# Reordering the set-up of a short-convolution and max-out feed-forward kernel

## The chip, the core and the metric

The kernel runs on one core of a Trainium2 chip. A core has five engines, each with its own instruction queue that it works off in order: TensorE (PE in the profile; its weight loads are listed apart as PEld), VectorE (DVE), ScalarE (ACT), GpSimd (POOL) and SyncE (SP). Here SP issues nearly all DMAs; ACT issues one. Engines wait for each other and for DMAs through semaphores. The metric is the device time of one launch in microseconds, and less is better.

## What is computed

An input x of 8 sequences, 4160 tokens and 192 channels passes a causal convolution of 7 taps whose weights are a softmax over the taps, one set for each of 8 heads of 24 channels. The result goes, token by token, through a feed-forward layer that takes the maximum of three products and multiplies it by an output matrix.

```python
w = np.exp(w - np.max(w, axis=-1, keepdims=True))
w = w / (np.sum(w, axis=-1, keepdims=True) + 1e-09)          # [8 heads, 7 taps]
out = np.einsum('hk,bskhg->bshg', w, x_unf)                  # causal convolution, 7 taps
...
h = np.maximum(np.maximum(x @ w1, x @ w2), x @ w3)           # x: 33280 x 192, w: 192 x 768
return (h @ w_out).astype(np.float32)                        # w_out: 768 x 192
```

## The kernel before

The 33280 tokens are cut into 65 blocks of 512. The maximum of three is made of two: the kernel forms the differences `wd` = w1 - w3 and w2 - w3, multiplies the convolved tokens by them, takes max(relu(first), second), and adds the w3 part through a product of w3 and w_out (`m16`), so PE has two instead of three large products for a block.

All order is written out by hand (the framework's scheduler is off): each engine does its instructions in the order in which the program names them. After a set-up for the weights and for four blocks, a loop over the blocks 2 to 64 does for each: the first-layer products (`l1`), the maximum (`top`: relu on ACT at line 490, maximum on DVE at line 491), the output products of the block before (`st2`), the convolution of a later block, and its transposes and loads.

The set-up, in the order of the program, with the names that the change touches:

- The filter `wk` is loaded by a DMA that ACT issues (line 230). SP issues x block 0 (`load_x(0)`, two DMAs), the first 256 columns of the weights (`load_wa`, `load_wb`), x block 1, the rest of the weights, `wos` (w_out) and x blocks 2 and 3.
- `keep_warm(n)` issues n matmuls on zeros (line 252).
- The softmax is made of a maximum on DVE (`wneg`), an exp on ACT (line 269; the engine loads a function table before it), and a sum, a reciprocal and a product on DVE, which write `line`, the taps in a row of zeros.
- From `line`, 38 small matmuls (line 283) build the banded matrix `band`, which ACT and DVE copy out of PSUM (line 287).
- Blocks 0 to 3 ("dense") are convolved by `conv_dense`: 80 matmuls (line 378) of `xz`, an fp16 copy of x in two zero-padded versions, against `band`; the halves n = 0 and n = 1 are cast to `yd` by two engines (line 383). `cast_dense` (line 211) makes `xz` out of the loaded `xf`.
- `zero_x(t)` zeroes partitions 32 to 63 of the x buffers of blocks 4, 5 and 6, which later loads fill only in part: on ACT by a copy of zeros (line 137), or on the engine that it is given by a memset (line 134). SP's loads into a buffer wait for it.
- `make_wd(n, j0, j1)` forms the difference number n for some of the six groups of 128 columns (line 302). `copy_w3` copies half of w3 to the other 64 partitions (line 306); the difference number 2, which holds the last 64 channels, needs it. `cross_wd` copies halves of `wd` (line 313).
- `l1_dense(tiles, parts)` issues the products of blocks 0 and 1: "F" are those of the first 128 channels (four full-array matmuls for two tiles; they need the ACT half of `yd`), "H" the third products, over the last 64 channels (half-array matmuls, which run in pairs; they need the other half of `yd` and `wd` number 2). `tops` follows with relu and maximum.

After the set-up, lines 676 to 704 give the order around the change: differences, `conv_dense(0)`, zero fill and loads of blocks 4 to 6, `copy_w3`, difference 2, x1's casts, F of block 0, `conv_dense(1)`, H of block 0 and its `tops`, then H and F of block 1, and so on with the next column groups. In `conv_dense(1)` DVE casts half 0 and ACT half 1, half 1 first.

Of the kernel before, what the change touches and what calls it, by code (L numbers as in the profile page):

```python
# [10 lines left out]
FP32 = mybir.dt.float32  # L11
FP16 = mybir.dt.float16
AXX = mybir.AxisListType.X
AF = mybir.ActivationFunctionType
# [14 lines left out]
def kernel(  # L29
# [83 lines left out]

    QUADS = 13
    assert (NB - QUADS) % 4 == 0
    xin, xbuf, XBUF, loaded = {}, [], 7, set()

    def get_x(t):

        if not 0 <= t < NB or t in xin:  # L120
            return
        if t < XBUF:
            xbuf.append(const.tile([P, NR, D], FP32, name=f"xf_{t}"))
        xf = xbuf[t % XBUF if t < NDENSE + XBUF else NDENSE + (t - NDENSE - XBUF) % 3]
        assert all(v[0] is not xf for v in xin.values())
        xin[t] = [xf, 0, ()]

    def zero_x(t, q0=0, q1=NR, eng=None):

        if t >= NDENSE:  # L130
            get_x(t)
        xf = xbuf[t]
        if eng is not None:
            eng.memset(xf[TOK:HALF, q0:q1, :], 0.0)
            return
        zero = idle[TOK:HALF, 0:D]
        nc.scalar.copy(out=xf[TOK:HALF, q0:q1, :],  # L137
                       in_=bass.AP(tensor=zero.tensor, offset=zero.offset,
                                   ap=[list(zero.ap[0]), [0, q1 - q0], [1, D]]))

    def load_x(t, eng=nc.sync):
        if not 0 <= t < NB:
            return
        loaded.add(t)
        get_x(t)
        xf = xin[t][0]
        if t < NDENSE:
            todo = [(0, c[3], c[1] * SEQ + c[2], i) for i, c in enumerate(chunks_of[t])]
        else:
            todo = [(HALF * (i // NR) + (0 if s else LAP), KR if s else TOK,  # L150
                     b * SEQ + s - (LAP if s else 0), i % NR) for i, (b, s) in enumerate(rows_of(t))]
        parts = []
        i, n = 0, len(todo)
        row = [c[2] for c in todo]
        while i < n:
            k = i
            while k + 1 < n and todo[k + 1][:2] == todo[i][:2] and row[k + 1] - row[k] == row[i + 1] - row[i]:
                k += 1
            step = row[i + 1] - row[i] if k > i else 0
            p0, rlen, _, q0 = todo[i]  # L160
            q1 = todo[k][3] + 1
            src = bass.AP(tensor=x.tensor, offset=row[i] * D,
                          ap=[[D, rlen], [step * D, q1 - q0], [1, D]])
            eng.dma_start(out=xf[p0:p0 + rlen, q0:q1, :], in_=src)
            if parts and parts[-1][0] == rlen:
                parts[-1] = (rlen, parts[-1][1], q1)
            else:
                parts.append((rlen, q0, q1))
            i = k + 1
        xin[t] = [xf, todo[0][0], parts]  # L170
# [28 lines left out]
    xz = {t: [const.tile([P, NQ, D], FP16, name=f"xz_{t}_{v}") for v in range(2)] for t in range(2)}  # L199
    xz[2], xz[3] = xz[0], xz[1]  # L200

    def cast_dense(t, copies, slots_=range(CYC // 32)):
        xf, _, parts = xin.pop(t)
        for v, copy in enumerate(copies):
            if copy is None:
                continue
            for s in slots_:
                cut = GRP * (32 * s // GRP + 1)
                a, b = (32 * s, cut) if v == 0 else (cut, 32 * s + 32)
                for (rl, q0, q1) in parts:  # L210
                    copy(  # L211
                        out=xz[t][v][0:rl, q0:q1, :].rearrange("p q (k c) -> p q k c", c=CYC)[:, :, :, a:b],
                        in_=xf[0:rl, q0:q1, :].rearrange("p q (k c) -> p q k c", c=CYC)[:, :, :, a:b])
# [14 lines left out]

    wk = const.tile([NHEAD, KW], FP32)
    nc.scalar.dma_start(out=wk[:], in_=weight)  # L230
    wos = const.tile([P, NJ, D], FP32)
    load_x(0)
    load_wa(slice(0, PW))
    load_wb(slice(0, PW))
    load_x(1)
    load_wa(slice(PW, 2 * PW))
    load_wb(slice(PW, DFF))
    load_wa(slice(2 * PW, DFF))
# [9 lines left out]
    def keep_warm(n, pool=psw, tag="w"):  # L248

        ps = pool.tile([P, NBLK], FP32, tag=tag, name="idle")  # L250
        for _ in range(n):
            nc.tensor.matmul(ps[:], lhsT=idle[:, 0:P], rhs=idle[:], start=True, stop=True)
# [6 lines left out]
    nc.vector.memset(line[:], 0.0)  # L259
    for v in range(2):  # L260
        nc.vector.memset(xz[0][v][:], 0.0)
    band = const.tile([P, NHEAD, BAND_W], FP16)
    nc.vector.memset(band[:], 0.0)
    keep_warm(5, psp, "p")
    wexp = const.tile([NHEAD, KW + 1], FP32)
    nc.vector.memset(wexp[:], 1e-9)
    wneg = const.tile([NHEAD, 1], FP32)
    nc.vector.reduce_max(out=wneg[:], in_=wk[:], axis=AXX, negate=True)
    nc.scalar.activation(out=wexp[:, 0:KW], in_=wk[:], func=AF.Exp, bias=wneg[:])  # L269
    wrec = const.tile([NHEAD, 1], FP32)  # L270
    nc.vector.reduce_sum(out=wrec[:], in_=wexp[:], axis=AXX)
    nc.vector.reciprocal(out=wrec[:], in_=wrec[:])
    zero_x(4)
    nc.vector.tensor_scalar_mul(out=line[:, 31:31 + KW], in0=wexp[:, 0:KW], scalar1=wrec[:])
    for v in range(2):
        nc.vector.memset(xz[1][v][:], 0.0)
    cast_dense(0, (nc.vector.tensor_copy, nc.vector.tensor_copy))
    CUT = 28
    for lo, hi, copy in ((0, CUT, nc.scalar.copy), (CUT, WIN, nc.vector.tensor_copy)):
        bps = psq.tile([32, hi - lo + 3, NHEAD], FP32, tag="q", name=f"band_{lo}")  # L280
# [5 lines left out]
        for a in range(4):  # L286
            copy(out=band[32 * a:32 * a + 32, :, 32 * a + lo:32 * a + hi],  # L287
                 in_=bps[:, 0:hi - lo, :].rearrange("p c h -> p h c"))
    zero_x(5)
    keep_warm(3, psp, "p")  # L290


# [7 lines left out]
    def make_wd(n, j0, j1, eng=nc.vector):  # L300
        f = slice(P * j0, P * j1)
        eng.tensor_sub(out=wd[:, n, f], in0=ws[:, n, f], in1=w3s[:, n // 2, f])

    def copy_w3(copy, j0, j1):
        f = slice(P * j0, P * j1)
        copy(out=w3s[HALF:P, 1, f], in_=w3s[0:HALF, 1, f])

    def cast_w3(j0, j1):
        f = slice(P * j0, P * j1)
        nc.gpsimd.tensor_copy(out=w3h[:, :, f], in_=w3s[:, :, f])  # L310

    def cross_wd(i, copy):
        copy(out=wd[HALF * i:HALF * (i + 1), NC, :], in_=wd[HALF * (1 - i):HALF * (2 - i), i, :])
# [52 lines left out]
    def conv_dense(t, copies, pools=((None, None),) * 2, order=(0, 1)):  # L366


        yd = dense[t] = ydp.tile([P, NC, NBLK], FP16, tag="yd", name=f"yd_{t}")
        for n in order:  # L370
            slots_ = ((0, 1, 2, 3), (4, 5, 4, 5))[n]
            pool, tag = pools[n]
            ps = (pool or psw).tile([P, NBLK], FP32, tag=tag or "w", name=f"D{n}_{t}")
            for (q, b, row_lo, rlen, lo, hi, cc) in chunks_of[t]:
                for v in range(2):
                    for g, s in enumerate(slots_):
                        h = (32 * s + 31 * v) // GRP
                        nc.tensor.matmul(  # L378
                            ps[32 * g:32 * g + 32, lo:hi],
                            lhsT=xz[t][v][0:rlen, q, 32 * s:32 * s + 32],  # L380
                            rhs=band[0:rlen, h, cc:cc + hi - lo],
                            start=(v == 0), stop=(v == 1), tile_position=(0, 32 * g))
            copies[n](out=yd[:, 2 * n, :], in_=ps[:])
# [129 lines left out]
    def l1_dense(tiles, parts="FH"):  # L513

        meet()
        for n, part in enumerate(parts):
            for t, j, pools in tiles:
                for i, (pool, tag) in enumerate(pools):
                    if (t, j, i) not in open_ps:
                        open_ps[t, j, i] = pool.tile([P, NBLK], FP32, tag=tag, name=f"l{tag}{i}_{t}_{j}")  # L520
                        begun.discard((t, j, i))
                    if part == "F":
                        a, b = wd[:, i, P * j:P * (j + 1)], dense[t][:, 0, :]
                    else:
                        a, b = w_of(i, NC - 1, j), y_all(t, i, NC - 1)
                    nc.tensor.matmul(open_ps[t, j, i][:], lhsT=a, rhs=b,  # L526
                                     start=(t, j, i) not in begun, stop=(t, j, i) in begun)
                    begun.add((t, j, i))

    def tops(*tiles):  # L530
        for t, j in tiles:
            top(t, j, (open_ps[t, j, 0], open_ps[t, j, 1]))
# [143 lines left out]
    GP = nc.gpsimd.tensor_copy  # L676
    make_wd(0, 0, 2)
    make_wd(1, 0, 2)
    zero_x(6, 4, NR, nc.vector)
    conv_dense(0, (ACT, DVE))  # L680
    zero_x(6, 0, 4)
    for t in range(NDENSE, XBUF):
        load_x(t)
    copy_w3(DVE, 0, 2)
    make_wd(2, 0, 2)
    cast_dense(1, (GP, ACT), (1, 2, 0))
    l1_dense([(0, 0, PQ), (0, 1, PQ)], "F")
    cast_w3(0, 2)
# [2 lines left out]
    for n in range(NC):  # L691
        make_wd(n, 4, 6, nc.gpsimd)
    cast_w3(2, 6)
    conv_dense(1, (DVE, ACT), order=(1, 0))
    make_wd(0, 2, 4)
    make_wd(1, 2, 4)
    cross_wd(0, GP)
    GP(out=wo[:], in_=wos[:])
    l1_dense([(0, 0, PQ), (0, 1, PQ)], "H")
    tops((0, 0), (0, 1))  # L700
    l1_dense([(1, 0, WW), (1, 1, WW)], "HF")
    tops((1, 0), (1, 1))
    l1_dense([(0, 2, PQ), (0, 3, PQ)], "FH")
# [130 lines left out]
```

## Time and profile before

| | us |
|---|---|
| median of 3 runs | 454.24 (454.09 to 456.25) |
| the profiled execution | 454.51 |
| its span, first to last instruction | 452.70 |
| PE busy in the span | 446.8 (99%) |
| DVE, ACT, POOL busy | 356.5, 320.0, 202.9 |

By stages, from the view of busy times in stretches of the span:

| stretch, us | what it holds | PE busy | DVE | ACT | POOL | DMA share |
|---|---|---|---|---|---|---|
| 0 to 7.29 | softmax, band, matmuls on zeros | 4.83 | 4.79 | 4.54 | 1.01 | 0.57 |
| 7.29 to 10.96 | conv 0, F of block 0 | 3.60 | 3.15 | 3.52 | 1.36 | 1.08 |
| 10.96 to 22.66 | conv 1, products of blocks 0 and 1 | 11.70 | 8.71 | 9.06 | 9.96 | 0.97 |
| 22.66 to 31.18 | conv 2 and 3, block 2 | 8.12 | 5.14 | 5.79 | 5.48 | 0.68 |
| 31.18 to 452.70 | the loop | 418.60 | 334.75 | 297.07 | 185.12 | 0.69 |

The busy time of an engine says how much of a stretch it spent in instructions, not whether the end of the stretch waited for it; for that the chain of waits and the timeline are read, whose lines give start, duration, engine, line, operation, tiles and, in brackets, the idle time before and what ended it. Tile names in the lines are output<-inputs; "x5" is a count of merged instructions.

### The profile page before, as it was taken

The page shows a single profiled execution, that of the slowest core. Times are in us where ns is not written, and L with a number is a line of the kernel's source. Part 1 is how long each engine was busy: PE and PEld are TensorE (multiplying, and loading weights), DVE is VectorE, ACT ScalarE, POOL GpSimd, SP SyncE. Part 2 cuts the span into 40 slices and gives each one's busy share as a digit, 9 for nine tenths or more (in the row PEclk, how much of TensorE's full clock was granted, in tenths as well). Part 3 has the DMA queues.
Part 4 walks back from the last instruction along what each step waited for, and adds up shares of the span by engine and source line. Part 5 has one row for each costly group of instructions (what it writes and reads, how often), then busy time and mean ns, then how long its engine had stood idle before and what let it go on. Part 6 is the DMA issues. An engine that isn't in the chain of part 4 may idle for free.

```text
span 452.7 us, 18493 instructions
## 1 busy us (share of the span) xinstructions
PE 446.8 (99%) x7702; PEld 412.6 (91%) x7702; DVE 356.5 (79%) x617; ACT 320.0 (71%) x604; POOL 202.9 (45%) x226
## 2 busy tenths in 40 slices
PE   7999999999999999999999999999999999999997
PEld 3569999999999999999999999999999999999996
DVE  7768778878878787887878788887878788787775
ACT  7767767767777676777767777776767777776664
POOL 2864836556454534645263464535346452505000
PEclk9999999999999999999999999999999999999999
DMA  7969997596875869587685949657594776535223
GB/s 205 231 178 166 199 205 195 146 206 180 169 180 147 168 129 207 138 176 185 118 190 141 210 117 184 177 136 186 133 206 124 178 189 118 117 89 104 59 72 106
DMA packets 127987, 72.03 MB, mean 159 GB/s; under 512 B 52064, under 2 KB 127711, under 8 KB 127903
## 3 DMA queue, kind: packets, MB, share of 16 engines
q1 hardware_dynamic: 127743, 70.75, 68.3%
q8 instruction: 60, 0.98, 1.0%
q14 instruction: 24, 0.20, 0.1%
q10 hardware_dynamic: 160, 0.10, 0.1%
HBM read 33.28 MB, written 25.56 MB: 130 GB/s over the span
## 4 chain that ended last, share of the span: by engine, by line
PE 97%; ACT 1%; DMA 0%; DVE 0%; issue 0%; ACTq 0%
PE po L567 36%; PE lq L503 31%; PE lp L503 22%; PE G L357 3%; PE lw L526 1%; PE lp L526 1%; PE D L378 1%; PE po L625 0%; PE po L598 0%; DMA wk<-in_weight_dram 0%; PE lq L526 0%; ACT xf L137 0%; ACT band L287 0%; ACT L269 0%; PE pm L337 0%; PE band L283 0%
## 5 line engine op out<-in xcount | busy, mean ns | idle before, releaser
L491 DVE TENSOR_TENSOR h<-r,lq 128x512 f16<-128x512 f16 x384 | 263.0, 686 | 85.1 <-ACT r L490 77.3
L567 PE MATMUL po<-wo,h 64*128 64x192 f16 x3024 | 329.8, 243 | 0.0
L490 ACT ACTIVATE r<-lp 128x512 f16<-128x512 f32 x384 | 229.0, 597 | 114.3 <-PE lp L503 100.8
L503 PE MATMUL lp<-yp,wd 64*128 64x512 f16 x1098 | 295.6, 376 | 0.0
L503 PE MATMUL lq<-yp,wd 64*128 64x512 f16 x1098 | 295.5, 376 | 0.0
L567 PEld LDWEIGHTS <-h 64*128 64x128 f16 x3024 | 240.9, 94 | 6.3 <-issue 4.1
L503 PEld LDWEIGHTS <-wd 64*128 64x128 f16 x2268 | 177.7, 94 | 10.6 <-issue 0.2
L194 POOL CAST x<-xf 103x768 f16<-103x768 f32 x122 | 97.5, 827 | 106.6 <-DMA xf<-in_x_dram 93.0
L567 PE MATMUL po<-m,yp 64*128 64x192 f16 x720 | 141.0, 243 | 0.0
L420 POOL COPY yp<-yp 64x1536 f16<-64x1536 f16 (+1 forms) x62 | 89.6, 1445 | 96.2 <-DMA yp<-ys 75.9
L575 DVE TENSOR_TENSOR o<-a,po 128x384 f32<-128x384 f32 x126 | 69.0, 547 | 0.0
L567 PEld LDWEIGHTS <-yp 64*128 64x128 f16 x720 | 66.3, 94 | 0.5
L574 ACT COPY a<-po 128x384 f32<-128x384 f32 x126 | 59.5, 472 | 0.0
L397 ACT CAST ys<-G 128x384 f16<-128x384 f32 x61 | 26.3, 482 | 9.5 <-PE G L357 9.4
L397 DVE CAST ys<-G 128x384 f16<-128x384 f32 x61 | 31.0, 550 | 0.0
L357 PE MATMUL G<-x,band 39*32 39x192 f16 (+2 forms) x1152 | 17.3, 234 | 0.0
L357 PEld LDWEIGHTS <-band 39*32 39x32 f16 x1152 | 10.7, 91 | 5.2 <-issue 4.7
L503 PE MATMUL lp<-yd,wd 64*128 64x512 f16 x36 | 9.7, 376 | 0.0
L503 PE MATMUL lq<-yd,wd 64*128 64x512 f16 x36 | 9.7, 376 | 0.0
L526 PEld LDWEIGHTS <-wd 128*128 128x128 f16 (+1 forms) x48 | 3.2, 98 | 5.7 <-issue 2.4
L211 POOL CAST xz<-xf 112x160 f16<-112x160 f32 (+2 forms) x15 | 4.1, 319 | 7.7 <-DMA xf<-in_x_dram 7.7
L378 PEld LDWEIGHTS <-xz 112*32 112x32 f16 x320 | 4.6, 107 | 2.7 <-issue 1.0
(74 smaller groups left out, 98.2 us busy)
## 6 DMA issues: line engine op xcount, KB each, us to landing
xf<-in_x_dram SPq DMA_DIRECT2D x113, 234.0 KB
out_dram<-o SPq DMA_DIRECT2D x62, 384.0 KB
xf<-in_x_dram SPq DMA_DIRECT2D x7, 204.8 KB
xf<-in_x_dram SPq DMA_DIRECT2D x3, 420.0 KB
ws<-in_moe_w_dram SPq DMA_DIRECT2D x8, 128.0 KB
yp<-ys SPq DMA_TRANSPOSE x62
out_dram<-o SPq DMA_DIRECT2D x5, 192.0 KB
wos<-in_moe_w_out_dram SPq DMA_DIRECT2D x1, 576.0 KB
```

The costliest lines, as they stand in the source:

```text
L194: nc.gpsimd.tensor_copy(out=x16s[t0][0:K, :, :, u, r, :].rearrange("p h j c -> p j h c"), in_=xf[0:K, 4 * r:4 * r + 4, :].rearrange("p j ( ...
L357: nc.tensor.matmul(G[2 * (k // per) + i][TOK * j:TOK * (j + 1), k % per, :], lhsT=band[row, h, HALF * i + LAP:HALF * i + KR], rhs=x16s[t0] ...
L378: nc.tensor.matmul(ps[32 * g:32 * g + 32, lo:hi], lhsT=xz[t][v][0:rlen, q, 32 * s:32 * s + 32], rhs=band[0:rlen, h, cc:cc + hi - lo], star ...
L397: copy(out=slots[t][:, i % 2, :, :, GRP * h0:GRP * (h0 + per)].rearrange("p u r (h c) -> p h (u r) c", c=GRP), in_=G[i][:].rearrange("p h ...
L420: nc.gpsimd.tensor_copy(out=yp[HALF * i:HALF * (i + 1), 1, :, :, :, :].rearrange("p i u k n -> p (i u k n)"), in_=yp[HALF * (1 - i):HALF * ...
L490: nc.scalar.activation(out=r[:], in_=ps[0][:], func=AF.Relu)
L491: nc.vector.tensor_max(out=hs[t][:, j, :], in0=r[:], in1=ps[1][:])
L503: nc.tensor.matmul(ps[i][:], lhsT=w_of(i, c, j), rhs=y_all(t, i, c), start=(n == 0), stop=(n == NC - 1))
L526: nc.tensor.matmul(open_ps[t, j, i][:], lhsT=a, rhs=b, start=(t, j, i) not in begun, stop=(t, j, i) in begun)
L567: nc.tensor.matmul(ps[b0, i][:, s % 2, :], lhsT=a, rhs=b, start=first, stop=last)
L574: nc.scalar.copy(out=a[:], in_=ps[s - 1, 0][:])
L575: nc.vector.tensor_add(out=outs[t][:, s - 1:s + 1, :], in0=a[:], in1=ps[s - 1, 1][:])
```

## The change

Six things move; what is computed stays.

1. A one-element exp on ACT stands before the real one, right behind the issue of the `wk` load, so that the function table is loaded there. The memset of `band` and `keep_warm(5)` are named after the real exp.
2. x block 1 is loaded by a DMA of ACT, after the exp, instead of by SP between two groups of weights.
3. The buffers of blocks 4 and 5 and half of block 6's are zeroed by GpSimd memsets instead of by ACT copies and a DVE memset; one of the two `xz` versions of block 1 is zeroed by GpSimd too.
4. x block 0 is cast in two parts, chunks 0 and 1 and then 2 to 4, as its two DMAs bring them: twelve casts instead of six.
5. `copy_w3` for the first columns goes from DVE to GpSimd and, with difference number 2, ahead of `conv_dense(0)`.
6. H of block 0 and its `tops` go ahead of `conv_dense(1)`; the cast of `wo` on GpSimd goes ahead of `cross_wd(0)`.

```diff
-        if t < XBUF:
-            xbuf.append(const.tile([P, NR, D], FP32, name=f"xf_{t}"))
+    xbuf = [const.tile([P, NR, D], FP32, name=f"xf_{t}") for t in range(XBUF)]
...
-    def cast_dense(t, copies, slots_=range(CYC // 32)):
-        xf, _, parts = xin.pop(t)
+    def cast_dense(t, copies, slots_=range(CYC // 32), qs=(0, NQ)):
+        xf, _, parts = xin[t]
+        parts = [(rl, max(a, qs[0]), min(b, qs[1])) for rl, a, b in parts if a < qs[1] and b > qs[0]]
+        if qs[1] == NQ:
+            xin.pop(t)
...
     nc.scalar.dma_start(out=wk[:], in_=weight)
+    warm = const.tile([1, 1], FP32)
+    nc.vector.memset(warm[:], 0.0)
+    nc.scalar.activation(out=warm[:], in_=warm[:], func=AF.Exp)
     wos = const.tile([P, NJ, D], FP32)
     load_x(0)
     load_wa(slice(0, PW))
     load_wb(slice(0, PW))
-    load_x(1)
...
-    band = const.tile([P, NHEAD, BAND_W], FP16)
-    nc.vector.memset(band[:], 0.0)
-    keep_warm(5, psp, "p")
     wexp = const.tile([NHEAD, KW + 1], FP32)
...
     nc.scalar.activation(out=wexp[:, 0:KW], in_=wk[:], func=AF.Exp, bias=wneg[:])
+    band = const.tile([P, NHEAD, BAND_W], FP16)
+    nc.vector.memset(band[:], 0.0)
+    keep_warm(5, psp, "p")
...
-    zero_x(4)
+    load_x(1, nc.scalar)
     nc.vector.tensor_scalar_mul(out=line[:, 31:31 + KW], in0=wexp[:, 0:KW], scalar1=wrec[:])
-    for v in range(2):
-        nc.vector.memset(xz[1][v][:], 0.0)
-    cast_dense(0, (nc.vector.tensor_copy, nc.vector.tensor_copy))
+    for t in (4, 5):
+        zero_x(t, eng=nc.gpsimd)
+    nc.gpsimd.memset(xz[1][0][:], 0.0)
+    nc.vector.memset(xz[1][1][:], 0.0)
+    zero_x(6, 4, NR, nc.gpsimd)
+    GP = nc.gpsimd.tensor_copy
+    cast_dense(0, (nc.vector.tensor_copy,) * 2, qs=(0, 2))
+    cast_dense(0, (nc.vector.tensor_copy,) * 2, qs=(2, NQ))
...
-    zero_x(5)
     keep_warm(3, psp, "p")
...
-    zero_x(6, 4, NR, nc.vector)
+    copy_w3(GP, 0, 2)
+    make_wd(2, 0, 2)
     conv_dense(0, (ACT, DVE))
...
-    copy_w3(DVE, 0, 2)
-    make_wd(2, 0, 2)
     cast_dense(1, (GP, ACT), (1, 2, 0))
...
+    l1_dense([(0, 0, PQ), (0, 1, PQ)], "H")
+    tops((0, 0), (0, 1))
     conv_dense(1, (DVE, ACT), order=(1, 0))
     make_wd(0, 2, 4)
     make_wd(1, 2, 4)
+    GP(out=wo[:], in_=wos[:])
     cross_wd(0, GP)
-    GP(out=wo[:], in_=wos[:])
-    l1_dense([(0, 0, PQ), (0, 1, PQ)], "H")
-    tops((0, 0), (0, 1))
```

## The prediction

> **What bounds the kernel now.** I read the page first: span, busy shares, slices.
>
> ```profile
> span 452.7 us, 18493 instructions
> PE 446.8 (99%) x7702; PEld 412.6 (91%) x7702; DVE 356.5 (79%) x617; ACT 320.0 (71%) x604; POOL 202.9 (45%) x226
> PE   7999999999999999999999999999999999999997
> ```
>
> TensorE (PE) is busy 99% of the span; only the first and the last slice are below 9. The change touches nothing after block 1, so only the set-up, the first 14 us, can give or lose time, and whatever shift reaches PE there is carried to the end. Next I read the chain of waits in order of time, for that stretch:
>
> ```profile
> 0.75 1.69 DMA wk<-in_weight_dram
> 2.50 1.28 ACT L269
> 3.80 0.31 ACT wexp L269
> 4.50 0.23 DVE line L274
> 4.78 0.94 PE band L283 x28
> ...
> 7.14 1.48 ACT xf L137
> 8.64 0.59 ACT yd L383
> 9.27 0.58 PE lp L526
> ```
>
> The filter weights land, ScalarE (ACT) only then loads its exp table (1.28 us), computes exp, VectorE (DVE) makes `line`, PE makes the band. At 7.14 a zero fill of an x buffer on ACT (1.48) stands in front of the cast `yd` that block 0's first products wait for. Last, the timeline by engine:
>
> ```profile
> 7.29 1.91 PE L378 MATMUL D<-band,xz 112*32 112x103 f16 x80
> 10.08 0.63 PE L526 MATMUL lp<-yd,wd 128*128 128x512 f16 x1
> 10.96 1.11 PE L378 MATMUL D<-band,xz 112*32 112x103 f16 x80
> 11.65 0.59 ACT L383 CAST yd<-D 128x512 f16<-128x512 f32 x1 [0.78 <-PE D L378]
> 13.18 1.41 PEld L526 LDWEIGHTS <-wd 128*128 128x128 f16 x8 [0.64 <-issue]
> 14.06 0.38 PE L526 MATMUL lp<-yd,wd 128*128 128x512 f16 x1
> ```
>
> The same 80 convolution matmuls take 1.91 us at 7.29 and 1.11 at 10.96; one 128x512 product takes 0.63 at 10.08 and 0.38 at 14.06. So PE runs at half speed up to about 10.8 (the clock row shows full speed from the start; the durations contradict it). I measure the shift at 13.18, the first full-array product of block 1: from there PE has no idle time before 28.28.
>
> **The change part by part.** *Table early.* The load depends on nothing once a one-element exp stands in front: it starts when ACT has issued the wk load (0.75+0.58 = 1.33) and ends at 2.61; the one-element exp, at most the 0.30 of the real one, ends by 2.9. wk has landed at 2.44, the maximum takes 0.14, so the real exp runs about 2.85 to 3.15 instead of 3.80 to 4.10. The band memset (0.51) now fills DVE's wait and ends at 3.15. From exp to `line` the rows take 0.62: 4.10 to 4.72, so 3.15 to 3.75. Gain 0.95.
>
> *x0 cast in two parts.* Six casts at 0.15 apart (0.92 in all) become twelve of half the size; by the spread of 0.182 (80 elements) to 0.266 (240) nearly all of it is fixed cost, so about 1.43, or 0.5 more. One memset of xz moves from DVE to GpSimd (POOL): 0.46 less. The two cancel: DVE still needs about 2.5 us from `line` to the band casts that conv 0 waits for (4.72 to 7.23). Conv 0 could start at 6.35 instead of 7.29, if nothing blocks DVE.
>
> *Zero fills on POOL.* ACT loses 1.47 and 1.48, the second one on the chain; DVE loses 0.70 (L134). POOL gets four memsets at 1.7, where it was idle until 9.39. Price by POOL's own memsets: 0.10 for 128x1, 0.21 for 128x128, 0.25 for 7x192, so 0.105 plus 0.76 ns an element: 1.27 twice, 0.83 (960), 0.69 (768), with gaps 4.25; POOL is free at about 5.95. Bounds: 0 extra, if all stays under its idle time, and 1.2 ns an element (the 64x512 copy, 0.61), which ends at 7.6. Behind them wait the w3 copy (half of 0.61) and, in DVE's order, the third difference `wd` and the cast of conv 0's second half; those are due only at 8.2, so either end is covered.
>
> *What POOL and DVE do to each other.* The trace shows one pair:
>
> ```profile
> 23.98 0.37 DVE L389 COPY yd<-yd 64x512 f16<-64x512 f16 x1 [2.37 <-ACT yd L383]
> 24.38 0.29 DVE L389 COPY yd<-yd 64x512 f16<-64x512 f16 x1
> 22.61 1.60 POOL L194 CAST x<-xf 103x768 f16<-103x768 f32 x2
> ```
>
> The first copy, while a POOL cast runs until 24.21, takes 0.37; its equal with POOL idle 0.29. It ends 0.14 after POOL's cast. L306's copy at 10.01 (0.38) also ends 0.14 after POOL's last xz cast (10.25). So such DVE operations appear to wait for the POOL operation in progress. The x0 casts (4.2 to 5.7) now fall into POOL's memsets. Bounds: 0, and all four memsets first: casts from 5.95 to 7.4, band casts, conv 0 at 8.1. I take one wait of 0.1, as in the rows, for each of four memsets: 0.4; conv 0 at 6.75. The Trainium skill (SBUF — State Buffer, "Who interferes with whom") says that a two-port DVE operation and a GpSimd operation exclude each other, the later one blocking fully. It speaks against this change: by that rule alone conv 0 would stand anywhere up to the 8.1 above.
>
> *x1 issued by ACT.* One DMA issue, 0.58, goes behind exp: 3.15 to 3.73; behind it ACT's band casts wait for PE until about 4.75, so it is hidden (0.58 on the path if not). SP loses the step from 5.06 to 5.69: every later weight, wos and x load is issued 0.63 earlier. x1 took 4.2 us from issue to its first use (5.06 to 9.39, a wait for that DMA), so it lands near 7.4.
>
> *Clock.* Before, PE paused from 3.52 to 4.78 and the clock rose about 6 us after it resumed. Now the pause is 3.55 to 3.8. Bounds: 10.8 as before, if something else than the pause set it, and before conv 0. If so short a pause does not count, work is continuous from 1.26 and the same 6.0 us end at 7.3, which I take. The Trainium skill (TensorE: Matmul & The Clock Gate, "The HAM clock gate") gives a free-running window of 3.4 us that must be busy; one window before 10.8 is 7.4, and with its phase unknown the rise would lie between 4.7 and 8.1; the sum would move by 0.4 at most. No row here shows the phase.
>
> *Third products (H) of block 0 ahead of conv 1.* Same PE work, new waits. Then: conv 0 6.75 to 8.1 (slow to 7.3), ACT's cast 7.7 to 8.3, block 0's first products (F) 8.35 to 9.2 (4 matmuls, 0.216 apart), DVE's cast done 8.9, H 9.3 to 9.73. ACT: zero fill 0.83 to 9.19, x1 casts 0.8 to 10.0; conv 1 9.95 to 11.05. Now r0, r1 (1.08) stand ahead of conv 1's cast on ACT: 10.0 to 11.1, cast to 11.7, so block 1's H starts at 11.75 with PE idle 0.7, where before H of block 0 filled that time. DVE: two maxima (1.28) from 10.6, its conv 1 cast 11.85 to 12.5, F of block 1 at 12.5 against 13.18. The sum: **0.7 gained**; 1.0 without the 0.4 at the casts.
>
> *Where it could stick.* POOL's first difference waits for weights until 13.40 and ends, a fourth of 2.79 later, at 14.1; its user on PE comes at 15.05, 0.9 of cover, plus the 0.63 of SP. POOL's x2 casts end half-way through 19.22 to 22.46, at 20.8, conv 2 starts at 22.66. wo is cast before its copy now; 19.28 against 20.59. All wider than 0.7. The rest of the kernel keeps its order, its loads follow PE.
>
> The profiled execution took 454.51, 1.81 more than its span of 452.70; the median 454.24 lies 0.27 below. 452.70 - 0.7 + 1.81 - 0.27 gives 453.5.
>
> **The rivals.** *B, the clock rises no sooner* (0.25). For it: 8-row band matmuls may not count as work. Conv 0 6.35 to 8.3, F slow to 10.06, H 10.15, conv 1 11.1, F of block 1 at 13.3 (+0.1), or 0.3 later with DVE's waits: what the front gains the new order gives back. 454.4.
>
> *C, slower: POOL's memsets hold off the x0 casts* (0.12). For it: the two copies above; against: those waits were of 0.1. Place: DVE between `line` and band. Conv 0 at 8.1, PE idle 6.4 to 8.1, longer than the pause before, and the clock rises about 6 us after, at 14.1. Slow conv 0 to 10.0, F to 11.75, H to 12.7, conv 1 to 14.6, then cast and H: F of block 1 at 15.8, 2.6 late: 456.8. It decides from a conv 0 later than about 7.4.
>
> *D, the clock is full before conv 0 and DVE is never held* (0.15). Conv 0 6.35 to 7.46, F at 7.7, H 8.65, conv 1 9.3, F of block 1 at 11.75: 1.4 gained; 2.2 if ACT's x1 casts and r0, r1 come free sooner. 452.0 to 452.8.
>
> *The table load comes no sooner* would leave 0.95 of it out; against it: nothing of ACT stands ahead. It is inside B.
>
> **How the numbers follow.** Likeliest is A, the sum, with 0.48: 453.5, its own range 452.9 to 454.2. B 0.25, D 0.15, C 0.12. The range to 8 in 10 takes D and B whole with their unknown costs and leaves C out: 452.0 to 455.6. A measurement of this kernel can tell about 0.5% (2.3 us) from no change: faster means below 451.97, the lower end of D and luck, 0.12; slower above 456.5, C and a tail of B, 0.12; same 0.76.
>
> **What would show it.** Table load at about 1.3; `line` near 3.75; conv 0 near 6.75 (7.4 or later: C); conv matmuls turning from 24 to 14 ns apart within conv 0 (not until 10.8: B); x0 casts on DVE longer than 0.2 while POOL's memsets run; ACT's conv 1 cast behind r0 and r1, PE idle before block 1's H; steady blocks at the same length as before. Wrong altogether would be a change of the pace after 31 us.

## The result, and the profile after

| | before | after |
|---|---|---|
| median, us | 454.56 (453.66 to 456.25, 16 runs) | 456.22 (455.73 to 457.82, 16 runs) |
| ratio | | 1.0035, 95% interval 1.0023 to 1.0047 |
| the profiled execution | 454.51 | 457.82 |
| its span | 452.70 | 456.0 |

The change costs about 1.6 us where 0.7 us of gain were forecast. The loss is below the 0.5% that the prediction called no change, but its interval holds neither 1.000 nor the forecast. The profiled execution is the slowest of the 16, so its trace shows more loss (3.3 us of span) than the median has; below, sizes of whole kernels are taken from medians, places and single waits from traces.

First the page of the kernel after: the span, the busy line of PE, its row of forty slices, and a row of the DMA queues (packets, MB, share) that will matter.

```profile
span 456.0 us, 18500 instructions
PE 448.7 (98%) x7702; PEld 412.6 (90%) x7702; DVE 358.0 (79%) x621; ACT 317.1 (70%) x603; POOL 208.1 (46%) x231
PE   7899999999999999999999999999999999999997
q8 instruction: 60, 0.98, 1.0%
```

The second slice of PE (11.4 to 22.8 us) now shows 8: PE stands idle later in the set-up than before. The timeline of the kernel after, by engine:

```profile
1.38 1.28 ACT L235 ACT_TABLE_LOAD   x1 [1.38 <-PEq L825]
...
1.73 2.69 POOL L133 MEMSET xf<- 32x1536 f32 x2
...
2.37 0.35 ACTq L163 DMA_DIRECT2D xf<-in_x_dram  x1
...
3.46 0.98 DVE L278 TENSOR_SCALAR line<-wexp,wrec 8x7 f16<-8x7 f32 x1
...
4.11 2.67 DVE L213 CAST xz<-xf 112x96 f16<-112x96 f32 x12
4.47 0.90 POOL L281 MEMSET xz<- 128x960 f16 x1
...
5.43 0.75 POOL L133 MEMSET xf<- 32x768 f32 x1
...
7.47 1.91 PE L386 MATMUL D<-band,xz 112*32 112x103 f16 x80 [0.39 <-DVE band L296]
...
12.79 0.37 PE L534 MATMUL lp<-yd,wd 64*128 64x512 f16 x1 [1.37 <-DVE yd L391]
...
13.33 1.11 PE L386 MATMUL D<-band,xz 112*32 112x103 f16 x80
...
14.81 3.36 PE L534 MATMUL lw<-yd,wd 64*128 64x512 f16 x8 [0.38 <-ACT yd L391]
...
17.97 0.53 PE L534 MATMUL lp<-yd,wd 128*128 128x512 f16 x1
```

Read it in order. The table load is early, as meant. Then `line` takes 0.98 us for 56 numbers; it ends at 4.44, just after POOL's second memset (1.73 + 2.69 = 4.42). The twelve x0 casts take 2.67 us beside the two other memsets. So conv 0 starts at 7.47, later than the 7.29 of before. H of block 0 follows only at 12.79, conv 1 at 13.33 (10.96 before), and the next full-array products after block 1's at 17.97 (14.06 before).

What stood in front of 12.79 is in the chain of waits of the kernel after, in order of time (start, duration, what):

```profile
4.43 6.58 DMA ws<-in_moe_w_dram
11.20 0.93 DVE wd L310
12.14 0.61 DVE yd L391
...
14.29 0.49 ACT yd L391
14.81 3.36 PE lw L534 x8
```

The last of the *first* weights, issued at 4.43, takes 6.58 us. DVE makes the third difference `wd` from it at 11.20 and, queued behind that, the `yd` half that H needs. Before, nothing of this was on the chain. The last line shows one thing more: block 1's eight products (four half-array, then four full-array ones) take 3.36 us; the same eight took 1.78 before. The view of stretches says why; its columns are the length, busy time (and instructions) of PE, PEld, DVE, ACT and POOL, the granted clock, the DMA share and GB/s:

```profile
11.44:14.86 3.42, 1.69 (x86) 1.29 (x88) 2.33 (x4) 1.56 (x3) 2.23 (x5) 1.00 0.61 162
...
14.90:18.20 3.30, 3.30 (x9) 0.78 (x9) 2.65 (x5) 1.01 (x2) 2.71 (x5) 0.50 0.93 268
```

The clock had risen at 11.44 by the trace's clock records, PE was then busy for only 1.69 of 3.42 us, and the clock was halved for 3.41 us (14.86 to 18.27). That costs about 1.6 us here (3.36 against 1.78). The other fifteen executions were granted 0.999 or 1.000 of the clock and this one 0.995, so the second fall is this execution's own.

When a transfer has landed, by the last of its semaphore updates in the trace (us from the span's start; "first weights" are the six transfers that SP issues between 1.7 and 5):

| kernel | first weights, first to last | x1 issued | x1 landed | x block 6, the last load of the set-up |
|---|---|---|---|---|
| before | 4.97 to 6.70 | 5.06 (SP) | 9.27 | 26.86 |
| after | 5.69 to 11.01 | 2.37 (ACT) | 10.27 | 29.85 |

x1 was issued 2.7 us earlier, landed 1.0 later, and held up all the rest. Lost, then, are about 3.9 us of front in this trace; of these 0.6 come back in conv 3, where the kernel before has a stall (0.40 us of idle PE at 28.28, the time that the prediction names) and this one has not. Without the second fall of the clock about 3.3 - 1.6 = 1.7 us would be left, an estimate from this one trace that lies close to the median's loss. That stall turned out to be the second half of the story.

### The profile page after: what moved, and what is told of

It reads as the page before. It is cut to its first block, busy times and chain, and to the rows that moved or that the text cites. A ratio compares the mean times of both kernels' runs of the same rounds, so it can differ in the third digit from the quotient of the medians.

```text
span 456.0 us, 18500 instructions
## 1 busy us (share of the span) xinstructions
PE 448.7 (98%) x7702; PEld 412.6 (90%) x7702; DVE 358.0 (79%) x621; ACT 317.1 (70%) x603; POOL 208.1 (46%) x231
## 4 chain that ended last, share of the span: by engine, by line
PE 96%; DMA 1%; SPq 1%; DVE 0%; ACT 0%; issue 0%; DVEq 0%
PE po L575 36%; PE lq L511 31%; PE lp L511 22%; PE G L365 3%; DMA ws<-in_moe_w_dram 1%; PE lw L534 1%; PE lp L534 1%; PE D L386 0%; PE po L633 0%; PE po L606 0%; SPq L225 0%; SPq L229 0%; PE pm L345 0%; ACT r L498 0%; DVE wd L310 0%; PE lq L534 0%
## 5 line engine op out<-in xcount | busy, mean ns | idle before, releaser
L534 PE MATMUL lw<-yd,wd 64*128 64x512 f16 (+1 forms) x24 | 6.6, 457 | 0.4 <-ACT yd L391 0.4
```

The costliest lines, as they stand in the source:

```text
L534: nc.tensor.matmul(open_ps[t, j, i][:], lhsT=a, rhs=b, start=(t, j, i) not in begun, stop=(t, j, i) in begun)
```

## The experiments

All ratios are against the kernel before on the same chip, with 95% intervals. Theories at the start: the loss comes from x1's early start (first weights late); or from GpSimd's fills holding DVE; or from the new order of the third products, which makes PE wait.

| run | what it is | median, us | ratio |
|---|---|---|---|
| e1_x1_on_sp | after, x1 back on SP | 455.79 | 1.0023 (1.0013 to 1.0033) |
| e2_zeros_back | after, fills back on ACT and DVE | 458.07 | 1.0082 (1.0069 to 1.0095) |
| e3_both_back | after, both back | 454.99 | 1.0013 (1.0003 to 1.0023) |
| e4_before_x1_act | before, x1 on ACT alone | 457.33 | 1.0066 (1.0053 to 1.0079) |
| e5_three_back | e3, H behind conv 1 again | 454.22 | 0.9990 (0.9979 to 1.0000) |
| e11_three_back_again | e5 once more | 455.01 | 1.0003 (0.9990 to 1.0015) |
| e6_tops_later | e3, block 0's maxima later | 454.63 | 0.9999 (0.9985 to 1.0012) |
| e7_x1_early_sp | after, x1 early, but on SP | 455.52 | 1.0026 (1.0013 to 1.0039) |
| e9_x2_before_wos | e5, x2 loaded ahead of `wos` | 455.40 | 1.0010 (0.9989 to 1.0031) |
| e10_h_back | after, H behind conv 1 again | 456.26 | 1.0048 (1.0029 to 1.0066) |
| e12_x6_later | e5, x block 6 loaded later | 456.64 | 1.0042 (1.0026 to 1.0059) |
| e13_before_x6_later | before, x block 6 loaded later | 457.03 | 1.0053 (1.0040 to 1.0065) |
| e15_h_back_x6_later | e10, x block 6 loaded later | 457.70 | 1.0067 (1.0054 to 1.0080) |

### Taking parts back: e1, e2, e3

e1 gives x1 back to SP in its old place, e2 gives the zero fills back to ACT and DVE, e3 does both.

```diff
# e1
-    load_x(1, nc.scalar)
...
     load_wb(slice(0, PW))
+    load_x(1)
     load_wa(slice(PW, 2 * PW))
# e2
-    for t in (4, 5):
-        zero_x(t, eng=nc.gpsimd)
-    nc.gpsimd.memset(xz[1][0][:], 0.0)
-    nc.vector.memset(xz[1][1][:], 0.0)
-    zero_x(6, 4, NR, nc.gpsimd)
+    zero_x(4)
+    for v in range(2):
+        nc.vector.memset(xz[1][v][:], 0.0)
```

> The changed kernel with x block 1 again issued by SP in its old place, all else as changed. Theory T (x1, issued by ACT at 2.37 us, shares the DMA engines with the first weights, which then land 2 to 4 us late): the first weights land by 6.7 again, the differences on DVE no longer wait for a DMA, and the time falls by 1.5 to 3 us against the changed kernel, to 453.3 to 454.7. Rival P (GpSimd's memsets, which hold up the product that makes line and the x0 casts, are the loss): conv 0 stays near 7.4 and the time stays near 456. Rival O (third products of block 0 ahead of conv 1 make new waits): stays near 456, with block 1's third products waiting for ACT.

> The changed kernel with the zero fills again on ACT and DVE, x1 still issued by ACT. T: conv 0 starts near 6.5 instead of 7.47, but the differences still wait for weights until about 11, so the time moves by less than 0.5 us from the changed kernel's 456.2. P: line at 3.75 and conv 0 a microsecond sooner bring the time to 455 or less, down to 454.5.

> The changed kernel with both taken back: x1 on SP, zero fills on ACT and DVE. What remains is the early table, the split casts of x0, the earlier w3 copy and the third products of block 0 ahead of conv 1. T and P together: conv 0 at 6.4 to 6.6, weights in time, 452.8 to 454.0, faster than before by up to 1.5 us. O: block 1 starts no sooner than before (13.2), PE idle some 0.6 us between conv 1 and block 1, 454.2 to 455.

e1 against e3 tells what GpSimd's fills do, with the weights in time in both. The timeline of e1:

```profile
4.09 2.92 DVE L213 CAST xz<-xf 112x96 f16<-112x96 f32 x12
...
7.70 1.91 PE L386 MATMUL D<-band,xz 112*32 112x103 f16 x80 [0.62 <-DVE band L296]
```

and of e3:

```profile
3.46 0.22 DVE L278 TENSOR_SCALAR line<-wexp,wrec 8x7 f16<-8x7 f32 x1
...
4.62 1.33 DVE L213 CAST xz<-xf 112x96 f16<-112x96 f32 x12
...
6.64 1.91 PE L385 MATMUL D<-band,xz 112*32 112x103 f16 x80 [0.32 <-DVE band L294]
```

The same twelve casts take 2.92 us beside the fills and 1.33 without; `line` 0.99 and 0.22. Conv 0 is 1.06 us later (7.70 against 6.64); in the medians 0.8 us are left (455.79 against 454.99), with intervals that overlap. In the two traces almost nothing is left at the end (spans of 453.3 both), because e3 pauses in conv 3 and e1 does not; that pause comes up again below. Neither run reached the range that theory T gave it (453.3 to 454.7 for e1, 452.8 to 454.0 for e3).

e2 against e3 tells what x1's early start does without fills on GpSimd: 458.07 against 454.99, 3.1 us, where T had expected e2 within 0.5 us of the changed kernel. One line of e2's timeline has it:

```profile
13.28 0.58 PE L533 MATMUL lp<-yd,wd 64*128 64x512 f16 x1 [2.39 <-DVE yd L390]
```

Conv 0 is as early as in e3 (6.63), the first weights land between 7.05 and 10.36, and PE stands idle for 2.39 us ahead of H; it runs at half clock until about 19. The two parts don't add: with the fills on GpSimd too, taking x1 back is worth only 0.43 us (456.22 against 455.79, at nearly the same times of before). The early conv 0 only makes PE wait longer for the weights. Two things add to e2's loss beyond the late weights: DVE's zero fill (0.70 us at 11.80) stands behind the late third difference and ahead of the `yd` half that H needs, and three of e2's five executions were granted only 0.992 to 0.996 of the clock, none of e3's twelve less than 0.999.

### x1 alone: e4, e7

e4 puts x1 on ACT's queue in the kernel before, behind the exp; besides, it allocates the x buffers at once, as the change does. e7 is the changed kernel with x1 as early, but on SP's queue, right behind x0.

```diff
# e4, in the kernel before
-    load_x(1)
...
+    load_x(1, nc.scalar)
     zero_x(4)
# e7, in the kernel after
     load_x(0)
+    load_x(1)
...
-    load_x(1, nc.scalar)
```

> The kernel before with one edit: x1 is issued by ACT behind the exp. Its DMA has to wait for a semaphore of an earlier weight DMA there, which landed at 4.97, so it is issued at about the time at which SP issued it (5.06), and the first weights are already on their way. T in the form that the early start does the harm: first weights land as before (by 6.7), time within 0.5 us of before's 454.5. T in the form that a second queue by itself does the harm, however late: later weights or x1 land 1 us and more later than before, time 455.5 or more.

> The changed kernel with x1 issued by SP right behind x0, all else as changed. Theory E (it is the early start of x1's 430 KB, not the second queue, that delays the first weights): weights of the first columns land 1.5 us or more later than the 5.0 to 6.7 of before, time 455.5 to 457. Rival Q (two queues that take turns on the engines do the harm): the weights are late by x1's own issue and transfer only, under 1.5 us, x1 lands before 7, and the time is under 455.8.

e4 loses 2.9 us, but in another way. Its timeline:

```profile
5.74 0.35 ACTq L163 DMA_DIRECT2D xf<-in_x_dram  x1
6.13 1.47 ACT L136 CAST xf<-idle 32x1536 f32<-32x1536 f16 x1 [2.38 <-DMA ws<-in_moe_w_dram]
```

Here the issue fell to a completion semaphore that a weight transfer of SP still held. ACT waited for that transfer until 5.74, and its zero fill and band casts waited behind; conv 0 came at 9.05. The first weights (5.13 to 6.76) were in time. So a DMA issued by a computing engine can stop that engine; the prediction had counted 0.58 us of issue and called it hidden.

In e7 x1 lands at 7.78 and the first weights only at 8.28 to 9.55: on one queue, too, x1's 420 KB hold them up by 3 us. On ACT's own queue both are later still (x1 10.27, weights to 11.01). e7 and e1 are the same within their intervals (1.0026 and 1.0023): with the fills on GpSimd in both, weights that come 3 us late cost nothing that these medians can show.

### The order of the third products: e5, e6, e10

e5 is e3 with H of block 0 and its maxima back behind conv 1, so of the change only the early table, the split casts and the w3 copy on GpSimd remain. e6 is e3 with H where the change puts it, but the maxima behind conv 1 and the differences 0 and 1 of the next columns. e10 is the changed kernel with H back, x1 on ACT and the fills on GpSimd.

```diff
# e5 (on e3) and e10 (on after)
-    l1_dense([(0, 0, PQ), (0, 1, PQ)], "H")
-    tops((0, 0), (0, 1))
     conv_dense(1, (DVE, ACT), order=(1, 0))
...
     cross_wd(0, GP)
+    l1_dense([(0, 0, PQ), (0, 1, PQ)], "H")
+    tops((0, 0), (0, 1))
# e6 (on e3)
-    tops((0, 0), (0, 1))
     conv_dense(1, (DVE, ACT), order=(1, 0))
     make_wd(0, 2, 4)
     make_wd(1, 2, 4)
+    tops((0, 0), (0, 1))
```

> As the kernel with x1 on SP and the zero fills on ACT and DVE (454.99), and also the third products of block 0 after conv 1 again; left are the early table, the split casts and the earlier w3 copy. Theory O (the order costs PE the 0.42 and 0.37 us that it waits for the casts of conv 1): those waits go, block 1's first full products start by 13.2 or sooner, 454.0 to 454.5, 0.4 to 0.8 below 454.99. Rival X (x1's landing near 10 sets conv 1 whatever the order): same within 0.3 us of 454.99.

> As the kernel with x1 on SP and the zero fills on ACT and DVE, third products of block 0 still ahead of conv 1, but its relu and maximum named after conv 1's casts and the differences for the next columns. O: PE no longer waits for the casts of conv 1, block 1's first full products start at 12.7 to 12.9; then DVE's maxima come later and may hold the next tiles to about 14.1, as before the change. 453.8 to 454.6. X: no change from 454.99.

> The changed kernel with block 0's third products and their maxima behind conv 1 again; x1 on ACT's queue and the zero fills on GpSimd stay. Theory E (x1's early start makes the first weights late and sets block 1): third products aren't ready before x1 is, so their order is worth little: 455.6 to 456.4 against 456.2 for the changed kernel; conv 1 starts when x1's casts are done, about 11, instead of 13.3. Theory H (the new order costs as much here as in e3 against e5, 0.8 us): 455.2 to 455.6. If x1's start had no part in it, with the order undone only the zero fills would be left: about 455.0.

In e3 PE waits 0.42 us for ACT's `yd` and 0.37 for DVE's ahead of block 1, because r0, r1 and two maxima of block 0 stand before those casts. e6 leaves 0.22 of it, e5 nothing. From e3 the ratio falls by 0.0023 to e5 and by 0.0010 to e11, the same kernel: 0.5 to 1.0 us, with overlapping intervals for e11. And here the first surprise: e5 starts block 1's full-array products, and the `lp` that follows them, 1.04 us earlier than the kernel before and is no faster. The timeline of e5:

```profile
13.02 0.38 PE L533 MATMUL lp<-yd,wd 128*128 128x512 f16 x1
...
26.77 0.97 PE L385 MATMUL D<-band,xz 112*32 112x103 f16 x67
...
28.97 0.34 PE L385 MATMUL D<-band,xz 112*32 112x103 f16 x13 [1.23 <-issue]
```

13.02 stands against 14.06. The clock is not the reason: e13, with the front of before and a clock that rose at 9.22 (8.96 in e5, 10.79 in the kernel before), has 13.95 there. At conv 2 half of the gain goes (its input is cast by GpSimd, which waits for x2). Conv 3 then starts 0.54 us earlier than before, 26.77 against 27.31, and after 67 of its 80 matmuls PE stands still for 1.23 us with no wait that the profile can name ("issue"). The last 13 start at 28.97; before, at 28.68.

e10 is the second surprise. The timeline of e10:

```profile
14.04 0.38 PE L534 MATMUL lp<-yd,wd 128*128 128x512 f16 x1
...
27.29 0.96 PE L386 MATMUL D<-band,xz 112*32 112x103 f16 x67
...
30.68 0.34 PE L386 MATMUL D<-band,xz 112*32 112x103 f16 x13 [2.42 <-issue]
```

Its first weights are late too (5.41 to 9.66), but with H behind conv 1 that costs block 1 nothing: it runs exactly when it did before the change. Yet its median is that of the changed kernel, 456.26. In this trace the loss begins with 2.42 us of "issue" after the same 67th matmul (30.68 against 28.68). The view of stretches has the rest:

```profile
27.77:31.18 3.41, 0.99 (x62) 0.75 (x52) 0.81 (x2) 0.81 (x2) 2.87 (x5) 1.00 0.98 222
31.18:34.60 3.42, 3.42 (x32) 1.84 (x26) 2.01 (x4) 1.08 (x2) 0.47 (x1) 0.50 0.41 126
```

PE was busy for 0.99 of the 3.41 us up to 31.18, and then the clock was halved for 3.41 us, as in the changed kernel's trace; this takes another 1.5 of the 3.5 us by which e10's span is longer than that of before.

### What stands still at conv 3: e11, e9, e12 to e15

Counted in the trace, the place is always PE's weight load number 480 (the first is 0). Behind block 1, the pauses without a named releaser that one trace has and another has not, above 0.25 us, stand at numbers 480, 608, 736, 863, 1374 and, once, 3801, in all seventeen traces: 127.7 apart, or a multiple of it. One place only does not fit (388, where e6 and e12 lose 0.5 and 0.3 us). The page row shown first fits: 60 packets of 16 KB on an "instruction" queue in one execution; 7,702 matmuls and as many weight loads are 15,404 instructions, some 257 for each packet, or 128 pairs. So PE's own program comes by DMA while the kernel runs, and I take the pause for PE waiting for its next packet. The packet that belongs to number 480, and what PE did (us):

| kernel | packet starts | ends | number 480 runs at | PE paused there |
|---|---|---|---|---|
| before | 25.82 | 27.10 | 28.68 | yes |
| e3 | 26.70 | 27.80 | 29.27 | yes |
| e5 | 26.33 | 27.55 | 28.97 | yes |
| e11 | 26.50 | 27.71 | 29.12 | yes |
| e10 | 27.81 | 29.13 | 30.68 | yes |
| e14 | 26.86 | 27.96 | 29.40 | yes |
| e12 | 24.57 | 26.00 | 28.03 | no |
| e13 | 24.33 | 25.33 | 28.10 | no |
| e15 | 24.76 | 25.69 | 28.49 | no |
| after | 28.66 | 29.80 | 32.00 | no |

Where PE paused, it went on 1.4 to 1.6 us after the packet's end, in six traces of six; in the other four it came 2.0 to 2.8 us after it. The seven traces not in the table have no pause there either (1.5 to 3.5 us). One time orders all seventeen: that from PE's weight load 375 to the packet's start. In no trace does the packet start before that load; where it starts 1.78 us or more behind it, PE pauses (the six), and where it starts up to 1.47 behind it, PE does not (the eleven). So the packet seems to be asked for about there. In the changed kernel PE came to that load only at 27.97 and the packet 0.69 later: there PE was late, not the packet.

What makes a packet late would be the loads of x, among which it seems to wait. Their end alone does not order the traces (29.34 in e11 and 29.35 in e10, with the packet 1.81 and 3.79 us behind load 375). It was tried by taking two loads out of its way: x block 6 is issued behind block 7.

```diff
-    for t in range(NDENSE, XBUF):
+    for t in range(NDENSE, XBUF - 1):
         load_x(t)
...
     load_x(7)
+    load_x(6)
```

e11 repeats e5; e9 tried on e5 to get x2 to conv 2 in time, by issuing it ahead of `wos` and casting it ahead of `wo`.

```diff
-    nc.sync.dma_start(out=wos[:], in_=moe_w_out.rearrange("(j p) c -> p j c", p=P))
     load_x(2)
+    nc.sync.dma_start(out=wos[:], in_=moe_w_out.rearrange("(j p) c -> p j c", p=P))
...
+    cast_dense(2, (GP, GP))
     GP(out=wo[:], in_=wos[:])
```

> The same kernel as e5_three_back: early table load, split x0 casts and the w3 copy on GpSimd stay; x1's load, the zero fills and block 0's third products are back in their old places. Theory F (what the front gains is lost again at conv 2 and conv 3, which wait for x2 and x3, because the loads of the set-up fill the DMA engines whatever the engines do): 453.7 to 454.9, within 0.2% of before; the first products of block 1 about 1 us earlier than before, at most 0.4 us of it left at 31 us. Theory G (the loss between 20 and 31 us was an accident of that one execution): about 453.6, ratio 0.998, and about 1 us earlier from block 1 on to the end.

> e5_three_back with x2's load issued ahead of wos, and GpSimd's casts of x2 ahead of the cast of wo. Theory F: x2 lands near 16.9 instead of 20.3, conv 2 no longer waits for GpSimd's casts (0.5 us regained), the shift at 26 us is about -1.0; the idle time inside conv 3, whose cause is not shown, decides the rest: 453.2 to 454.5. Theory G: no difference from e11. A third theory (wos late holds the output products of the first blocks instead): PE waits for wo near 20 us, 454.5 to 455.5.

> e5_three_back with the load of x block 6 (two DMAs, first used near 40 us) issued behind that of block 7, so that the loads of the set-up end about 2 us earlier, near 25.5. Theory I (TensorE's own instructions come by DMA, 16 KB for 256 rows; the packet for the rows from conv 3's 68th matmul on waits behind the loads of x, so conv 3 can't end before about 28.7 whatever the front does): the packet starts at 24 to 25.5 instead of 26.3, no idle time or less than 0.3 us inside conv 3, 453.2 to 453.9, 0.998 of before. Theory J (the stall has another cause): the stall stays, 454.2 to 455.

> The kernel before with the same move of x block 6's load alone. Theory I: the idle 0.40 us inside conv 3 goes, 0.3 to 0.4 us gained: ratio 0.999. Theory J: no difference.

> The same kernel as e10_h_back, one more execution. If its time is lost to the instruction packet as in e10 (the load of weights and x ends only at 29.4 us there), PE stands still in conv 3 for 1 us or more again, and block 1's products again begin when they did before the change. If e10's 2.4 us were an accident, the loss of 1.6 us must show elsewhere: late first weights, conv 1 later than 11.5.

> e10_h_back with x block 6's load later as in e12. Theory I: the packet comes earlier, the stall inside conv 3 shrinks, 455 to 455.8 against 456.26. Theory J: 456.0 to 456.5.

e11 starts block 1 0.93 us earlier than the kernel before and ends 1.26 later: the gain is lost at conv 2 and at number 608 (0.68 us idle). So e5's loss was no accident. e9 moved the wait instead: x2 landed at 16.57, `wos` at 20.32, and PE waited 1.84 us for `wo`. In these two orders the loads of the set-up were the bound, and their order chose who waited.

With x block 6 later, the packet starts at 24.3 to 24.8 in all three kernels, 0.3 to 0.9 us behind load 375, and the pause at number 480 is gone in all three: this part of the theory held. The gain that it forecast did not come: later packets now come late, perhaps because the moved loads fall on them. The timeline of e12:

```profile
27.28 1.10 PE L385 MATMUL D<-band,xz 112*32 112x103 f16 x80
...
34.00 0.26 PE L574 MATMUL po<-wo,h 64*128 64x192 f16 x2 [1.27 <-issue]
```

Conv 3 runs through in 1.10 us, and PE stands still at 34.00 instead, at number 608; e15 for 1.51 us at the same number and 0.46 at 736, e13 at 736, 863 and 1374 (0.68, 0.60 and 0.76); the last, at 73 us, is too late for the moved loads. All three lose 0.4 to 0.7%.

e14, one more execution of e10, took 457.21: block 1 0.3 us early, 1.31 us idle at number 480, 1.96 at number 1374 (74 us), and no second fall of the clock. So e10's pause at conv 3 is no accident either, though its size varies. e7 has 2.16 at 1374 as well.

e8_after_again was one more execution of the changed kernel itself:

> The changed kernel unchanged, for another profile: the first one is of its slowest execution (457.82 against a median of 456.22), with the clock back at half from 14.86 to 18.27. A usual execution should show the same late weights and the same wait of 1.4 us for DVE's cast, but no second fall of the clock, with block 0's next products near 16.

It took 458.19: first weights to 10.66, conv 0 at 7.47 and block 0's H at 12.40, near the first trace's 12.79, but no second fall of the clock; it rose only at 15.69, and the next products of block 0 came at 17.25 instead of the expected 16. Pauses at 736 and 1374 add to the front's loss.

## Why the prediction was wrong

Three terms of its sum failed: the wait of 0.4 us for GpSimd's memsets (measured: 0.8 to 1.1), the weights that were to go out 0.63 us earlier (they went out 3.3 later), and the carrying of every shift to the end (0.9 to 1.0 us of gain at block 1 were gone at 36 us).

1. **The table load early**: right. Start 1.38 and 1.28 us (1.33 and 1.28 forecast), and `line` would be done at 3.68 without the fills (e3), 1.04 us earlier than before; 0.95 was forecast.

2. **Twelve casts instead of six**: right in size, 1.33 us where nothing disturbs them, 1.43 forecast. Conv 0 without the fills at 6.64, forecast 6.35.

3. **POOL and DVE**: the mechanism was seen, the size was not. Taken were 0.4 us, a wait of 0.1 for each memset, from two short rows; measured are 1.06 us at conv 0 (e1 against e3) and 0.84 (the changed kernel against e2). The Trainium skill (SBUF — State Buffer, "Who interferes with whom"), by which conv 0 could be anywhere up to 8.1, was the better guide than the rows that I chose: 7.47 to 7.70. In the rows of before, the waits were short because DVE's operation came near the end of POOL's (23.98 against 24.21, 10.01 against 10.25). Rival C named this place rightly, and its sign, conv 0 later than about 7.4, came true; it priced the place at 2.6 us, and it cost 0.8 (e1 against e3, with overlapping intervals). That C's 456.8 lies near the measured 456.22 is luck.

4. **x1 issued by ACT**: the step that failed first. It said: "SP loses the step from 5.06 to 5.69: every later weight, wos and x load is issued 0.63 earlier", and x1 "lands near 7.4". It counted the issue and kept each transfer's time as it was. But the transfers slow each other down. x1's 420 KB, started at 2.37 among the first weights, took 7.9 us instead of 4.2, and the first weights up to 7.3 instead of 3.3. SP then waited for the completion of earlier transfers before it could issue more (1.6 and 1.4 us for two of them), so that the later weights went out 3.3 us later (8.98 against 12.24 for one w3 load), not 0.63 earlier. This part costs 3.1 us in e2 against e3, where conv 0 is early (with DVE's fill and the clock in it), and 0.4 in the changed kernel, where the fills hold conv 0 back; 0.4 is within the intervals.

5. **The clock**: the 7.3 of the forecast was wrong in every trace, and so was the prediction's span of 4.7 to 8.1 (the earliest rise is at 8.23); for the changed kernel (11.44 and 15.69) rival B was right. The rise came between 8.2 (e6) and 15.7 (e8), in e2 by the durations only at about 19, and always about 1.6 us or more after conv 0 had begun. Whether the shorter pause ahead of the band moved it can't be told: executions of one kernel differ by 0.7 us (e5 8.96, e11 8.31) to 4.2 (the changed kernel and e8). A second fall, worth about 1.6 us, was not foreseen; the prediction let the clock move the sum by 0.4 at most. The window of 3.4 us in the Trainium skill (TensorE: Matmul & The Clock Gate, "The HAM clock gate") agrees with the changed kernel's trace, where the clock was full for 3.41 us, half for 3.41 and full again. In all traces with clock records the stretches between two changes are whole multiples of 3.41 us (443.73 is 130 of them).

6. **H ahead of conv 1**: forecast were 0.7 us of idle PE ahead of block 1; e3 has 0.42 and 0.37, which is right. Not forecast was the other side: H needs the third difference, whose weights come last, so that in the changed kernel conv 1 and all behind it wait for the weights that point 4 made late. With H behind conv 1 (e10) the same late weights cost block 1 nothing.

7. **"Whatever shift reaches PE there is carried to the end"**: the step that failed last, and the reason why e5 and e11 do not gain. Of the 1.04 and 0.93 us that they are ahead at block 1, nothing is left at 36 us; e10 is level at block 1, 2.0 us late behind conv 3 and 3.5 at 36 us. Between lie the casts of x2, which wait for loads, PE's packet for number 480 (608 in e11) and, in e10, the half clock after it. The idle 0.40 us at 28.28 was in the trace of before; the prediction used it as the place up to which PE has no idle time, and did not ask why PE idles there.

The sum of losses, by taking the parts back in this order: after 1.0035, x1 back 1.0023, fills back 1.0013, order back 0.9990 and 1.0003. From the first to the last the intervals are apart, so that the three parts together carry the loss; each single step is about as wide as its interval, and another order gives other shares (e2 and e10 put one part back and are slower than, or level with, the whole change).

**What stays open.** That the packet for number 480 waits behind loads is concluded from moving x block 6, and that it is asked for near load 375 from its earliest start in seventeen traces; no row of a trace shows either. Why the packets at 1374 (74 us) come late in five traces is not known. How the median execution of the changed kernel divides its 1.6 us can't be read from two traces that are both slower than it: e8, without a second fall of the clock, lost 3.7 us. No version here beats the kernel before by more than its interval.

## What to carry to other kernels

A DMA that is issued earlier is not a DMA that lands earlier: in a stretch where the transfers are the bound, add up bytes by what is needed first, and give a later need no earlier start. A gain in a set-up counts only up to the next thing that comes at its own time, here loads and PE's own instructions; look for a short idle time without a cause behind the place of the gain, and count the instructions up to it. GpSimd work laid beside a chain of short DVE operations is paid for by that chain, even if GpSimd itself has time.

## What was not expected of the hardware

- PE's program arrives by DMA during the run, by the count of the 60 packets of 16 KB, and a packet that comes late seems to stop PE: 0.2 to 2.4 us, always at the same instruction numbers, 1.4 to 1.6 us after the packet's end where the one for number 480 was late.
- ACT's queue issued x1 at 2.37 while ACT was still loading its table (to 2.66), though the program names the real exp ahead of it; in e4 the same instruction waited until 5.74 for a weight transfer and stopped ACT.
- A DVE operation on 8x7 elements took 0.98 us instead of 0.22 beside a GpSimd memset.
- The clock fell to half for 3.41 us after a stretch of 3.4 us in which PE was busy for 1.69 (changed kernel) and for 0.99 (e10); the longest idle time within them was 1.37 and 2.42.
